# Agent attention and a maxout network: key turns in three parts, query turns in two, and head operations with places of their own

## The chip, the cores and the metric

The kernel runs on one core of a Trainium2 chip. The metric is device time in microseconds; the median of eight runs of the kernel before is 454.28 us (453.96 to 456.04).

## The reference

```python
def _attn_ref(q, k, v, agents):          # q, k, v: 4 x 12544 x 128; agents: 4 x 49 x 128
    def sm(a, b): ...                    # softmax(scale * a @ b^T) over the last axis
    a2k = sm(agents, k)
    agent_v = a2k @ v                    # 4 x 49 x 128
    q2a = sm(q, agents)                  # 4 x 12544 x 49
    return q2a @ agent_v

def _moe_ref(x, w1, w2, w3, w_out):      # x: 50176 x 128; w1..w3: 128 x 768; w_out: 768 x 128
    h = np.maximum(np.maximum(x @ w1, x @ w2), x @ w3)
    return h @ w_out
```

Everything is float32 outside; the kernel works in bfloat16 inside.

## The kernel before

For each of the four batches the kernel first goes through all keys and values (98 tiles of 128 rows, in eleven groups of nine or eight tiles) and sums exponentials and weighted values for the 49 agents. From the normalised sums `av` it makes a matrix G: agent values times the weights' differences w2 - w1 (columns from C21 = 0) and w3 - w1 (columns from C31 = 768; one block of 128 of them, the fourth, takes w3 - w2 instead), and a linear part through w1 and w_out. Then it goes through the queries, in 49 groups of 1024 rows. A query group is cast, turned, multiplied with the agents and exponentiated to `e_q`. For each of six blocks f of the hidden layer there is a first product u (`uv_ps`), a relu of it on ACT (`a_sb`, line 677), a second product v and a maximum of both on DVE (`r`, line 687); for f = 4 (FI) the two products are summed in one buffer and ACT does both steps (lines 674 and 685). Out of the six r tiles and w_out come the output's two halves (`o_ps`, lines 692 and 701), which DVE scales (line 708) and SP stores (line 715).

The order is written out by hand. Every operation is put into a list with a place, `at(place, fn)`; the list is sorted, and in that order the instructions are issued, so that each engine's queue is the sorted list cut down to its own instructions. A query group takes six place units. KEY holds the places of a group's steps relative to its start (6 s), LATE those of the groups from 36 on, OWN those of single groups, BORDER those around the change of batch, BATCH0 and BATCH3 those of a batch's last steps. Names: `u0` to `u5`, `v0` to `v5` products, `a` relus, `x` maxima, `oc` and `lin` output products, `sc` scaling, `st` store, `qt` and `qe` a query turn on PE and its evacuation, `s` and `ex` query scores and exponentials, `ks`, `ke`, `kv`, `ka`, `ea` the key group's scores, exponentials, values and sums.

Batch 0's keys and values are worked off in the head (function `head`), before any query group. There SP loads key group g at place g and value group g at g + 3.3; POOL casts a key group (line 378), PE turns it (365), DVE evacuates (368), PE takes scores (354), ACT exponentiates (359) and casts values (383), PE adds totals (395) and values (405), and from the third group on issues four matmuls that keep it busy (`warm(WARM)`, line 328). After the last key scores come twelve more (LAST_WARM), the differences of the weights (294), `av` (409), and G's two products (485) with their evacuations (418 on DVE, 420 on ACT). The places of the head are moved to the query groups' scale by adding HEAD_END - Z, about -16.32, so the head ends at 0.66.

The keys and values of batches 1 to 3 are worked off beside the query groups, one key group with each (function `k_group`). SP loads them, POOL casts them, and SP turns the keys through the DMA (`turn_k`, line 502); a few query groups (the last of each batch and all from 36 on) are turned through the DMA too (line 633). The places of loads, casts and turns come from STREAM, relative to 11 units ahead of the group (LEAD):

```python
STREAM = {"kl": 0.0, "ld": 0.5, "kc": 1.0, "qc": 1.5, "vl": 1.9, "kt": 2.0, "vc": 3.2}
...
z = 6.0 * s - LEAD + x
K[n] = (z if z > HEAD_END else HEAD_END + 0.001 * (s + x / 6.0)) - 6.0 * s
```

`kl`, `ld` and `vl` are the loads of keys, queries and values, `kc`, `qc` and `vc` their casts, `kt` the turn. What would fall into the head is put right behind it. Group 0's query load has place 13.15 on the head's scale, behind all but the last value load, and its cast 14.6, behind all key casts. SP issues all loads, DMA turns and stores (but the load of the agents) in one queue; after the first seven loads, all issued by 4.42 us, the next follows at 5.78, as earlier ones land.

Of the kernel before, what the change touches and what calls it, by code (L numbers as in the profile page):

```python
# [10 lines left out]
BF16 = mybir.dt.bfloat16  # L11
# [17 lines left out]
    "s": -2.94209, "ex": -2.10461, "u1": -0.58526, "a1": -0.11108, "u2": 2.13391, "a2": 3.22306,  # L29
    "v1": 3.39126, "u3": 3.76716, "x1": 4.61365, "v2": 4.65907, "u0": 4.68062, "a3": 4.76358,  # L30
    "x2": 4.9054, "a0": 5.15584, "v0": 5.44974, "u4": 5.62746, "x0": 6.09964, "a4": 6.12388,
    "u5": 6.27862, "v3": 6.63325, "a5": 6.82242, "v4": 6.98304, "x4": 6.98433, "lin1": 7.02719,
    "oc12": 7.03328, "sum": 7.23728, "oc10": 7.59283, "x3": 7.74792, "v5": 7.87225, "rec": 8.46283,
    "x5": 9.47889, "oc13": 9.6877, "oc11": 9.69832, "oc14": 10.58762, "oc15": 10.856, "lin0": 10.87306,
    "oc05": 11.17012, "sc1": 11.55345, "oc01": 11.72189, "oc00": 11.77009, "oc03": 11.79963,
    "oc02": 11.90624, "oc04": 11.95959, "sc0": 12.74339, "st": 15.47059,
# [3 lines left out]
        "u2": 0.64554, "u0": 0.6497, "a0": 0.75101, "a2": 0.92875, "sum": 1.27525, "u3": 2.06003,  # L40
        "v0": 2.59116, "x0": 2.68446, "a3": 2.85638, "rec": 2.96325, "u1": 3.03882, "v2": 3.6736,
        "u4": 4.24684, "a1": 4.93475, "x2": 5.01871, "v3": 5.81978, "u5": 5.84299, "a4": 5.908,
        "a5": 6.60823, "x3": 6.61479, "v4": 6.9759, "v5": 7.08557, "x4": 7.15158, "v1": 7.27894,
        "x5": 7.66161, "x1": 7.70792, "lin0": 9.14279, "oc05": 10.43605, "oc00": 10.7932, "oc02": 10.85481,
        "oc03": 11.37967, "oc01": 11.41219, "oc04": 11.66746, "sc0": 11.83826, "lin1": 12.49398,
        "oc10": 12.50239, "oc11": 12.59233, "oc12": 12.77266, "oc13": 12.88978, "oc14": 13.54796,
        "oc15": 13.60373, "sc1": 13.75975, "st": 20.17439,
    },
    1: {
        "qt": -4.60541, "qe": -4.48042, "s": -2.95099, "ex": -1.32724, "ks": 1.62294, "u0": 1.73602,  # L50
        "ke": 2.36058, "sum": 2.56616, "kv": 2.79082, "a0": 2.92319, "ka": 3.26757, "u2": 3.4201,
        "v0": 3.45964, "a2": 3.84717, "u3": 4.22117, "rec": 4.22129, "x0": 4.49406, "a3": 4.56793,
        "u1": 4.62522, "v2": 4.63012, "x2": 4.73195, "a1": 4.86854, "v3": 5.12545, "u4": 5.25359,
        "x3": 5.55542, "ea": 5.62671, "a4": 5.96399, "u5": 6.17953, "a5": 6.26476, "v1": 6.28947,
        "x1": 6.30399, "v4": 6.40498, "v5": 6.63853, "x5": 6.88027, "x4": 7.41578, "lin0": 8.99321,
        "oc00": 9.79175, "oc04": 10.56667, "oc02": 10.75084, "oc03": 11.28772, "oc01": 11.5494,
        "oc05": 11.68913, "sc0": 12.27589, "lin1": 12.53566, "oc13": 12.60573, "oc15": 12.61178,
        "oc10": 12.70709, "oc14": 13.24775, "oc12": 13.54581, "oc11": 13.80424, "sc1": 14.02652,
        "st": 19.02898,
    },  # L60
    34: {
        "qt": -2.58866, "qe": -1.82932, "s": -1.30778, "ex": -1.10174, "ks": 0.14415, "sum": 0.55608,
        "rec": 0.59015, "ke": 0.68278, "u0": 0.7058, "ea": 0.72143, "u2": 1.49989, "a0": 2.15219,
        "v0": 2.18384, "x0": 2.25012, "kv": 2.57078, "a2": 2.84672, "ka": 3.10787, "u3": 3.14749,
        "a3": 3.82134, "u1": 3.94172, "v3": 3.96473, "a1": 4.22804, "x3": 4.34837, "v2": 4.43956,
        "u4": 4.5536, "u5": 4.96643, "a4": 5.32988, "x2": 5.54314, "a5": 6.22364, "v4": 6.22498,
        "v1": 6.372, "x4": 6.51691, "v5": 6.61382, "x1": 6.73976, "x5": 6.95861, "lin1": 8.28778,
        "oc15": 8.36021, "lin0": 8.73553, "oc13": 9.18722, "oc04": 9.72211, "oc14": 10.51955,
        "oc01": 10.73827, "oc02": 10.8464, "oc03": 12.33286, "oc05": 12.39876, "oc00": 12.40014,
        "oc11": 12.72237, "sc0": 13.30654, "oc12": 14.30997, "oc10": 14.62572, "sc1": 14.9543,  # L70
        "st": 25.03309,
    },
    35: {
        "qt": -2.43671, "qe": -1.9414, "s": -1.5744, "ex": -1.28805, "ks": -1.09088, "ke": -0.64495,
        "sum": -0.18909, "kv": -0.10783, "ka": 0.5331, "rec": 0.56684, "u0": 0.82589, "a0": 0.91902,
        "u2": 1.00358, "v0": 1.49877, "x0": 1.58537, "a2": 2.26288, "u3": 2.5102, "v2": 2.57899,
        "x2": 3.98475, "u1": 4.05488, "a3": 4.05504, "v3": 4.37636, "a1": 4.49639, "u5": 4.62208,
        "x3": 4.92789, "a5": 5.44572, "v5": 5.48263, "x5": 5.93851, "u4": 7.30642, "a4": 8.24488,
        "v1": 8.30836, "x1": 8.49394, "lin0": 8.71742, "oc03": 8.91263, "oc02": 9.07857, "v4": 9.24912,
        "x4": 9.32541, "oc00": 9.39236, "oc04": 9.69131, "oc01": 10.88106, "lin1": 10.92225,  # L80
        "oc05": 11.01981, "oc15": 11.13488, "sc0": 11.61665, "oc12": 11.69455, "oc13": 11.87736,
        "oc14": 13.32657, "oc10": 13.37252, "oc11": 13.49981, "sc1": 13.74093, "st": 42.57773,
    },
    36: {
        "s": -4.45673, "ex": -3.49789, "u1": -0.09348, "a1": 2.12897, "u2": 2.20348, "a2": 2.77677,
        "v2": 3.2876, "u0": 3.526, "v1": 3.8727, "x2": 4.34512, "x1": 4.34975, "u3": 4.36198,
        "a0": 4.73186, "a3": 5.00514, "v0": 5.29756, "u4": 5.75498, "x0": 5.91535, "sum": 6.0162,
        "a4": 6.30588, "v3": 6.39331, "x3": 6.48929, "u5": 6.75132, "rec": 7.30888, "a5": 7.33831,
        "v4": 7.78698, "v5": 7.80684, "x5": 7.96407, "x4": 8.12232, "lin1": 9.0675, "oc12": 9.24639,
        "oc14": 9.95322, "oc10": 10.40131, "lin0": 10.43281, "oc04": 10.55626, "oc01": 10.64608,  # L90
        "oc11": 11.24862, "oc15": 12.02168, "oc13": 12.20592, "oc00": 12.38398, "oc03": 12.91102,
        "sc1": 12.98528, "oc02": 14.0029, "oc05": 14.08645, "sc0": 14.96085, "st": 29.7755,
    },
    37: {
        "s": -2.47874, "ex": -1.87009, "u1": -0.70419, "a1": -0.60046, "u2": 2.0221, "a2": 2.21078,
        "v2": 3.56807, "x2": 3.92118, "u0": 4.2218, "v1": 4.32407, "x1": 4.92454, "a0": 5.43373,
        "v0": 5.83985, "u3": 6.06605, "x0": 6.29959, "u5": 6.46966, "v3": 6.48031, "a3": 6.91113,
        "a5": 7.46701, "u4": 7.96938, "sum": 8.00459, "x3": 8.25588, "rec": 8.25634, "v5": 8.35007,
        "lin1": 8.44693, "oc11": 8.49987, "a4": 8.62997, "oc13": 8.8661, "v4": 9.25227, "x5": 9.45205,
        "oc12": 9.91769, "x4": 10.00657, "oc10": 10.0531, "lin0": 10.26202, "oc15": 10.56081,  # L100
        "oc14": 10.87787, "oc04": 10.95601, "oc05": 11.15532, "sc1": 11.49682, "oc01": 11.77199,
        "oc02": 11.78318, "oc00": 11.81904, "oc03": 12.16132, "sc0": 13.17137, "st": 43.83189,
    },
    47: {
        "s": -2.63303, "ex": -1.35705, "u1": -0.72334, "a1": -0.55161, "u2": 2.09887, "a2": 2.6128,
        "v1": 2.71229, "u3": 4.07931, "v2": 4.23837, "a3": 4.51758, "x1": 4.63092, "u0": 4.71212,
        "a0": 5.0718, "x2": 5.13888, "u4": 5.22695, "v0": 5.2509, "x0": 5.96934, "u5": 6.00235,
        "a4": 6.49548, "v3": 6.59342, "v4": 6.61016, "sum": 6.94315, "lin0": 6.95342, "x3": 6.98518,
        "a5": 7.11094, "oc00": 7.22404, "oc02": 7.24709, "v5": 7.29105, "rec": 7.33314, "x4": 7.43763,
        "lin1": 7.62467, "oc03": 7.73819, "oc11": 7.80383, "x5": 7.80889, "oc14": 8.24845, "oc12": 8.30273,  # L110
        "oc04": 8.48507, "oc10": 10.74469, "oc01": 11.20725, "oc05": 11.70935, "sc0": 11.81857,
        "oc15": 11.86159, "oc13": 12.01123, "sc1": 12.03976, "st": 16.08395,
    },
    48: {
        "s": -2.45577, "ex": -1.62439, "u1": -0.82051, "a1": -0.04899, "u2": 1.5047, "v1": 1.68501,
        "a2": 1.84167, "u0": 1.85869, "v2": 2.12726, "a0": 2.96358, "x1": 3.66201, "x2": 3.71048,
# [53 lines left out]
    },  # L170
}
BATCH0 = {
    "red": -0.0796, "tot": 0.34012, "nrm": 0.77389, "p31": 0.90693, "p21": 1.22633,
}
BATCH3 = {
    "red": -1.41636, "tot": -0.09802, "nrm": 0.57786, "p31": 0.95637, "p21": 1.99854,
# [4 lines left out]
def kernel(  # L181
# [26 lines left out]
    GT = 8  # L208
# [626 lines left out]
```

## Time and profile before

| | |
|---|---|
| median of eight runs | 454.28 us |
| the profiled execution, its own time | 456.04 us |
| its span, first to last instruction | 453.7 us (453.66) |
| busy share: PE, DVE, ACT, POOL | 96%, 89%, 88%, 37% |
| DMA queue 1's packets, share of 16 engines' time | 85.7% |
| first product of batch 0's G on PE | at 41.74 us |
| first maximum (r) on DVE | at 47.58 us |
| a query group from then on, with and without a key group | 8.15 and 7.71 us |

PE is TensorE, DVE VectorE, ACT ScalarE, POOL GpSimd, SP SyncE, PEld TensorE's weight loads. A row of the time line gives start and duration in us, the engine, the line and operation, out<-in with partitions x elements and type, the count, and in brackets the idle time before it and what ended that. A row of the waits gives the waiting engine and line, whom it waited for, the total in us, the times and the longest.

### The profile page before, as it was taken

How to read it: one execution, taken by the hardware profiler on the slowest of the kernel's cores; microseconds unless marked ns; L12 is line 12 of the kernel's file. 1: busy time of each engine (PE TensorE's matmuls, PEld its weight loads, DVE VectorE, ACT ScalarE, POOL GpSimd, SP SyncE). 2: the span in 40 equal slices, each digit the busy share in tenths (PEclk: the TensorE clock that was granted, in tenths of full speed). 3: DMA queues.
4: the chain of work that ended last, by engine and by line, in shares of the span. 5: the costliest groups of instructions: out<-in, count | busy, mean ns of one | idle time of the engine just before them, and what ended most of it. 6: DMA issues, size and time to landing. Idle time of an engine off the chain costs nothing.

```text
span 453.7 us, 13313 instructions
## 1 busy us (share of the span) xinstructions
PE 433.9 (96%) x5506; PEld 279.1 (62%) x5506; DVE 404.5 (89%) x505; ACT 398.4 (88%) x456; POOL 169.5 (37%) x165
## 2 busy tenths in 40 slices
PE   2988999999999999999999999999999999999995
PEld 2864566666665666666665666666665556565664
DVE  3324799999999999999999999999999999999995
ACT  1665899999998999999988999999989899999983
POOL 4335365556324354464423354544401101111000
PEclk9999999999999999999999999999999999999999
DMA  8999899898879989999799999999566666654933
GB/s 313 410 409 327 269 294 231 294 283 270 236 243 327 304 268 284 317 330 259 215 307 296 257 345 274 303 335 272 178 209 157 192 174 185 179 168 135 349 140 140
DMA packets 83655, 118.86 MB, mean 262 GB/s; under 512 B 57671, under 2 KB 59659, under 8 KB 83595
## 3 DMA queue, kind: packets, MB, share of 16 engines
q1 hardware_dynamic: 83392, 117.92, 85.7%
q8 instruction: 43, 0.70, 0.6%
q14 instruction: 17, 0.14, 0.1%
q10 hardware_dynamic: 203, 0.10, 0.1%
HBM read 78.74 MB, written 25.69 MB: 230 GB/s over the span
## 4 chain that ended last, share of the span: by engine, by line
PE 85%; DMA 8%; DVE 4%; issue 1%; ACT 1%; POOL 0%; DVEq 0%; SPq 0%
PE uv_ps L662 35%; PE o_ps L701 32%; PE o_ps L692 6%; DMA st<-in_k_dram 5%; PE m_ps L639 3%; PE m_ps L625 3%; DMA st<-in_q_dram 2%; DVE r L687 2%; PE m_ps L514 2%; PE m_ps L354 2%; DMA ag_st<-in_agents_dram 1%; PE m_ps L650 1%; PE uv_ps L485 1%; DVE o_sb L708 1%; PE o_ps L788 0%
## 5 line engine op out<-in xcount | busy, mean ns | idle before, releaser
L687 DVE TENSOR_TENSOR r<-uv_ps,a_sb 128x1024 bf16<-128x1024 f32 x245 | 297.5, 1222 | 10.5 <-PE uv_ps L662 5.5
L677 ACT ACTIVATE a_sb<-uv_ps 128x1024 bf16<-128x1024 f32 x245 | 242.9, 1024 | 20.2 <-PE uv_ps L662 16.9
L662 PE MATMUL uv_ps<-e_q,G 49*128 49x512 bf16 (+1 forms) x1248 | 182.6, 370 | 2.5 <-ACT G L420 1.0
L701 PE MATMUL o_ps<-wo_bf,r 128*128 128x128 bf16 x2352 | 179.1, 220 | 0.0
L701 PEld LDWEIGHTS <-r 128*128 128x128 bf16 x2352 | 139.8, 98 | 45.2 <-issue 42.2
L662 PEld LDWEIGHTS <-G 49*128 49x128 bf16 x1248 | 57.2, 94 | 63.4 <-issue 25.4
L620 POOL CAST q_bf<-st 128x1024 bf16<-128x1024 f32 x49 | 51.0, 1040 | 102.3 <-DMA st<-in_q_dram 82.3
L708 DVE TENSOR_TENSOR o_sb<-o_ps,recips 128x512 f32<-128x512 f32 x98 | 67.0, 685 | 2.9 <-PE o_ps L701 1.5
L498 POOL CAST v_bf<-st 128x1152 bf16<-128x1152 f32 (+1 forms) x33 | 37.5, 1137 | 47.8 <-DMA st<-in_v_dram 45.1
L685 ACT ACTIVATE r<-uv_ps 128x1024 bf16<-128x1024 f32 x49 | 50.3, 1026 | 1.3 <-PE uv_ps L662 0.6
L494 POOL CAST k_bf<-st 128x1152 bf16<-128x1152 f32 (+1 forms) x33 | 37.5, 1137 | 36.2 <-DMA st<-in_k_dram 36.2
L674 ACT ACTIVATE uv_ps<-uv_ps 128x1024 f32<-128x1024 f32 x49 | 49.6, 1011 | 0.9 <-PE uv_ps L662 0.6
L526 POOL TENSOR_TENSOR Eacc<-Eacc,e_k 128x441 f32<-128x441 f32 x27 | 27.7, 1024 | 39.7 <-ACT e_k L359 38.3
L692 PE MATMUL o_ps<-G,e_q 128*128 128x256 bf16 x196 | 37.9, 275 | 0.0
L645 ACT ACTIVATE e_q<-m_ps 128x512 bf16<-128x512 f32 x49 | 29.2, 597 | 2.3 <-PE m_ps L639 1.2
L629 DVE COPY qT<-m_ps 128x1024 bf16<-128x1024 bf16 x34 | 23.3, 686 | 3.4 <-PE m_ps L625 3.4
L368 DVE COPY kT<-uv_ps 128x1152 bf16<-128x1152 bf16 (+1 forms) x11 | 8.3, 752 | 17.2 <-PE uv_ps L365 17.2
L692 PEld LDWEIGHTS <-e_q 128*128 128x128 bf16 x196 | 12.1, 97 | 18.3 <-issue 18.1
L625 PE MATMUL m_ps<-ident,q_bf 128*128 128x128 bf16 x272 | 21.2, 222 | 0.1
L639 PE MATMUL m_ps<-qT,agT 128*64 128x512 bf16 (+1 forms) x104 | 19.9, 389 | 0.6 <-DVE qT L629 0.6
L378 POOL CAST k_bf<-st 128x1152 bf16<-128x1152 f32 (+1 forms) x11 | 12.5, 1137 | 17.9 <-DMA st<-in_k_dram 17.9
L383 ACT ACTIVATE v_bf<-st 128x1152 bf16<-128x1152 f32 (+1 forms) x11 | 12.2, 1112 | 7.9 <-DMA st<-in_v_dram 7.9
(73 smaller groups left out, 233.4 us busy)
## 6 DMA issues: line engine op xcount, KB each, us to landing
st<-in_q_dram SPq DMA_DIRECT2D x48, 512.0 KB, 5.5
out_dram<-o_sb SPq DMA_DIRECT2D x48, 512.0 KB, 5.4
st<-in_k_dram SPq DMA_DIRECT2D x40, 576.0 KB, 5.5
st<-in_v_dram SPq DMA_DIRECT2D x40, 576.0 KB, 8.6
st<-in_k_dram SPq DMA_DIRECT2D x4, 512.0 KB, 3.8
st<-in_v_dram SPq DMA_DIRECT2D x4, 512.0 KB, 6.7
st<-in_moe_w_dram SPq DMA_DIRECT2D x3, 384.0 KB, 10.7
kT<-k_bf SPq DMA_TRANSPOSE x33, 4.2
```

Of the source, the lines that this page charges most:

```text
L494: nc.gpsimd.tensor_copy(out=d["kb"][:, :n, :], in_=d["k"][:, :n, :])
L498: nc.gpsimd.tensor_copy(out=d["vb"][:, :n, :], in_=d["v"][:, :n, :])
L620: nc.gpsimd.tensor_copy(out=d["qb"], in_=d["q"])
L625: nc.tensor.transpose(t[:, j * P:(j + 1) * P], d["qb"][:, j, :], ident)
L662: nc.tensor.matmul(t[:, h, j0 * P:j1 * P], G[b][h * H:h * H + A, col + f * P:col + (f + 1) * P], d["e"][h * H:h * H + A, j0 * P:j1 * P], s ...
L674: nc.scalar.activation(u, u, AF.Relu)
L677: nc.scalar.activation(a_sb[f], u, AF.Relu)
L685: nc.scalar.activation(r, v_ps[f], AF.Relu)
L687: nc.vector.tensor_tensor(out=r, in0=v_ps[f], in1=a_sb[f], op=ALU.max)
L692: nc.tensor.matmul(t[:, i * 2 * C:(i + 1) * 2 * C], d["e"][:, jj * P:(jj + 1) * P], G[batch[jj]][:, C1O:C1O + 2 * C], start=(i == 0), stop ...
L701: nc.tensor.matmul(t[:, c:c + C], r_sb[f][:, h, jj * P:(jj + 1) * P], wo_bf[:, f, :], start=False, stop=True, skip_group_check=True)
L708: nc.vector.tensor_tensor(out=d["out"][:, j:j + m, :], in0=d["o", o].rearrange("p (j c) -> p j c", c=C), in1=d["r"][:, j:j + m].unsqueeze( ...
```

## The change

Key turns go through the DMA in three transfers instead of one, at places of their own; query turns by the DMA go in two. STREAM is now relative to the group's start and holds for every group: key loads at -16 instead of -11, key casts at -14 instead of -10, the three turns at -10.4, -9.95 and -9 with the query load before and the value load between them; nothing is held back to the head's end any more. Groups 0, 1 and 2 have places of their own for loads, casts and turns. The head's single operations have places in HEAD (relative to the place of the last key group, 13 on the head's scale). The weights: w3 is loaded right behind key load 1, the last 256 columns of w2 and all of w1 ahead of key load 6, the first 512 columns of w2 behind the last values. Query 0 is loaded behind key load 5 and cast ahead of key cast 3. LAST_WARM stands before the scores of key group 8. w2 - w1 is made on DVE alone, in two parts, and the evacuations of G's products have places of their own, the w3 part in two pieces on ACT for all batches. OWN, BORDER, BATCH0, BATCH3 and LATE have new values; KEY is the same.

```diff
+HEAD = {
+    "wl2": -11.95775, "wl1": -7.66522, "wl0": -7.00016, "w1c": -2.96197, "df": -2.63283,
+    "d21b": -2.16516, "wrm": -0.87406, "wl1b": 0.64663, "d31": 1.40444, "wol": 3.17448, "rcp": 3.42607,
+    "d21a": 3.71019, "nrm": 3.94714, "p31": 4.00522, "p21": 4.04405, "e31a": 4.05579, "e31b": 4.06804,
+    "e21b": 4.46718, "e21a": 5.31734, "woc": 6.19661, "w1t": 8.79656, "pli": 11.44809, "lin": 12.66141,
+}
+STREAM = {
+    "kl": -16, "kc": -14, "ld": -10.5, "kt0": -10.4, "kt1": -9.95, "qc": -9.5, "vl": -9.1, "kt2": -9,
+    "qd0": -8.95, "qd1": -8.45, "vc": -7.8,
+}
 OWN = {
     0: {
...
+        "ld": -11.22746, "qc": -10.38907, "qt": -6.32237, "qe": -5.87362, "s": -5.34845,
...
     1: {
...
+        "ld": -7.93803, "kl": -7.91068, "vl": -7.01176, "qc": -5.42752, "kc": -5.2794, "kt0": -5.26207,
+        "vc": -4.96613, "kt2": -4.66934, "kt1": -4.27484, "qt": -3.2266, "qe": -1.10869, "s": 0.42495,
...
+    2: {
+        "kl": -13.87399, "kc": -10.95348, "ld": -10.11466, "kt0": -8.29036, "qc": -8.07793,
+        "kt2": -7.5516, "kt1": -7.16622, "vl": -6.52325, "vc": -4.56598,
+    },
...
-    def load_w(i):
-        wst[i] = load_tile().rearrange("p j c -> p (j c)")[:, :Dff]
-        nc.sync.dma_start(wst[i], (moe_w1, moe_w2, moe_w3)[i])
+    def load_w(i, c0=0, c1=Dff):
+        if i not in wst:
+            wst[i] = load_tile().rearrange("p j c -> p (j c)")[:, :Dff]
+        nc.sync.dma_start(wst[i][:, c0:c1], (moe_w1, moe_w2, moe_w3)[i][:, c0:c1])
...
-    def differences_21():
-        difference(nc.vector, C21, 1, 0, slice(0, Dff // 2))
-        difference(nc.gpsimd, C21, 1, 0, slice(Dff // 2, Dff))
+    def difference_21(cols):
+        difference(nc.vector, C21, 1, 0, cols)
...
-            if g == NK + 1:
-                at(t + 0.1, lambda: load_w(0))
-                at(t + 0.2, lambda: load_w(2))
...
-        at(t - 0.65, lambda: load_w(1))
...
+        at(z + HEAD["wl0"], lambda: load_w(0))
+        at(z + HEAD["wl2"], lambda: load_w(2))
+        at(z + HEAD["wl1"], lambda: load_w(1, FI * P, Dff))
+        at(z + HEAD["wl1b"], lambda: load_w(1, 0, FI * P))
...
+        at(z + HEAD["p31"], lambda: product(C31))
+        at(z + HEAD["e31a"], lambda: evacuate(C31, 0, 2 * P))
+        at(z + HEAD["e31b"], lambda: evacuate(C31, 2 * P, Dff))
+        at(z + HEAD["p21"], lambda: product(C21))
+        at(z + HEAD["e21a"], lambda: evacuate(C21, 0, 2 * P))
+        at(z + HEAD["e21b"], lambda: evacuate(C21, 2 * P, Dff))
...
-        def turn_k():
-            d["kT"] = bf_tile("kT", 3)
-            nc.sync.dma_start_transpose(out=d["kT"][:, :n, :], in_=d["kb"][:, :n, :].rearrange("p j c -> p (j c)"))
+        def turn_k(i):
+            if i == 0:
+                d["kT"] = bf_tile("kT", 3)
+            j0, j1 = i * n // 3, (i + 1) * n // 3
+            nc.sync.dma_start_transpose(out=d["kT"][:, j0:j1, :],
+                                        in_=d["kb"][:, j0:j1, :].rearrange("p j c -> p (j c)"))
...
+        def turn_by_dma(i):
+            if i == 0:
+                d["qT"] = work.tile([P, GT, P], BF16, tag="qT", bufs=3, name="qT")
+            j0, j1 = i * n // 2, (i + 1) * n // 2
...
-        for n, x in STREAM.items():
-            z = 6.0 * s - LEAD + x
-            K[n] = (z if z > HEAD_END else HEAD_END + 0.001 * (s + x / 6.0)) - 6.0 * s
+        K.update(STREAM)
```

## The prediction

> **What bounds the kernel now.** I read the busy time by stage first, cut at the events that the change touches:
>
> ```profile
> 20.00:41.74 21.74, 18.88 (x305) 12.95 (x303) 8.16 (x14) 12.75 (x16) 7.13 (x7) 1.00 1.02 409
> 41.74:47.58 5.84, 4.87 (x38) 2.49 (x38) 2.13 (x5) 3.31 (x5) 3.38 (x3) 0.71 0.82 137
> 47.58:62.74 15.16, 14.58 (x184) 8.97 (x183) 13.81 (x18) 14.76 (x19) 7.35 (x7) 1.00 0.94 291
> 62.74:120.00 57.26, 57.26 (x760) 37.66 (x759) 56.55 (x71) 54.28 (x63) 33.70 (x33) 1.00 0.93 273
> ```
>
> After the stretch's bounds and length the columns are busy us of PE, PEld, DVE, ACT, POOL, then the granted clock, the DMA share, GB/s. Until 41.74 (first product of batch 0) the loads run at 409 GB/s: the head waits for memory. From 62.74 PE is busy all the time and DVE for 56.55 of 57.26: a query group takes 8.15 us (spacing of line 645's rows), and no load has a part in that. Between lies the ramp, 5.84 us without a single r tile.
>
> Then the time line of the head, POOL and PE, and the first steps on DVE:
>
> ```profile
> 9.98 1.15 POOL L378 CAST k_bf<-st 128x1152 bf16<-128x1152 f32 x1 [0.37 <-DMA st<-in_k_dram]
> ...
> 18.57 1.15 POOL L378 CAST k_bf<-st 128x1152 bf16<-128x1152 f32 x1 [1.71 <-DMA st<-in_k_dram]
> ...
> 38.14 1.04 POOL L620 CAST q_bf<-st 128x1024 bf16<-128x1024 f32 x1 [6.42 <-DMA st<-in_q_dram]
> ```
>
> ```profile
> 9.47 1.14 PE L365 MATMUL uv_ps<-ident,k_bf 128*128 128x128 bf16 x9
> ...
> 21.28 0.39 PE L354 MATMUL uv_ps<-agT,kT 128*128 128x49 bf16 x9
> 21.51 0.66 PE L365 MATMUL uv_ps<-ident,k_bf 128*128 128x128 bf16 x9
> ...
> 23.34 0.39 PE L354 MATMUL uv_ps<-agT,kT 128*128 128x49 bf16 x9
> ...
> 36.41 2.75 PE L328 MATMUL uv_ps<-ident 128*128 128x512 bf16 x12
> ...
> 41.74 0.52 PE L485 MATMUL uv_ps<-wall,avT 128*64 128x512 bf16 x4 [0.39 <-DVE avT L409]
> ```
>
> ```profile
> 47.58 1.22 DVE L687 TENSOR_TENSOR r<-uv_ps,a_sb 128x1024 bf16<-128x1024 f32 x1 [0.35 <-PE uv_ps L662]
> ```
>
> Key cast 3 runs at 9.98, cast 6 at 18.57: two 576 KB loads each 2.86 us. Query 0 is cast after all keys. Nine turns take 1.14 us early and 0.66 later: PE runs at half rate until 20.06. A round of PE (scores, turns, totals, values, four warming matmuls) is 23.34 - 21.28 = 2.06 us, shorter than the 2.86 between keys, so PE waits for loads and LAST_WARM's twelve fill a wait.
>
> Last, SP's own waits:
>
> ```profile
> SPq L502 <- POOL q_bf L620: 146.7, 25, 8.7
> SPq L633 <- POOL q_bf L620: 74.2, 15, 7.7
> ```
>
> SP stands 146.7 us before key turns, with loads behind them in its queue. But in all waits PE loses only about 3 us to casts (q_bf 1.8 + 0.8, Eacc 0.5). This standing is covered.
>
> **Steady part: nothing.** Key loads 5 place units sooner (6.8 us at 8.15 us for 6 units), 66 more key turns, 15 more query turns, loads between them. KEY's order on PE, DVE and ACT is untouched, LATE's engine orders are the same to a swap or two among line 701's steps, so the 8.15 and 7.71 us periods stay. Cover: SP issues per group one turn (1.30), two key/value loads, a query load and a store (0.58 + 0.43 + 0.45 + 0.38), 3.1 us of 8.15. If each third costs as much to issue as a whole turn, it is 5.7 us, in a turned query group 1.24 more: still hidden. Lower end none; the upper end is a third that lands one after the other, 3 x 4.2 = 12.6 us per group; the 6.8 us of earlier loading and SP's standing speak for the lower, which I take. The Trainium skill ("DMA: Bandwidth & Descriptors", "Rules for kernel authors") speaks against the cut: many small transfers should be made one large one. By its reason, fixed cost per transfer, 81 more would be a loss; the row of 4.2 us for a whole 288 KB turn and PE's full rows say that it is hidden here.
>
> **Head: the query cast blocks POOL.** Here I expect the change to hurt. Query 0's load goes behind key load 5, its cast (place -10.39) just ahead of key cast 3 (-10.32). POOL works in order. Query 0 is then the tenth load: 8 x 576 + 384 (w3, now after key 1) + 512 = 5504 KB. The ten loads before key cast 6 are 5760 KB and 18.57 us; 256 KB less at 1.43 us per 576 KB gives 17.93. Query cast 1.04, key cast 3 1.15: key group 3 is cast by 20.12 instead of 11.13, and keys 4 and 5, landed long before, queue behind it; on PE turns 3 and everything after stand.
>
> PE's queue from 20.12 to the last key scores: two rounds without warming at half rate, 2 x 2.37 (9.47 to 11.84 us, spacing of L365), 4.74; six with, 6 x 2.06 = 12.4; query 0's turns and scores, now in the middle, 0.62 + 0.41 = 1.0; LAST_WARM, moved ahead of scores 8, 2.6 of its 2.75. Sum 20.7: 40.9. Behind them on ACT, in order, the last exps 0.50, value casts 9 and 10, 1.16 + 0.63; then values 0.38, normalise 0.20, 0.3 of handing over: first product at 44.0 against 41.74, +2.3. Lower end -0.3: PE is in time and value load 10, which lands 0.33 later (131 KB of w2 cut off behind it, 262 left), plus cast, values and normalise make it 41.4. Upper end +4.0: the record has PE's clock change at 20.06, 43.95 and 47.37, on a grid of 3.41 us; if the second round fills no whole step, full rate comes 3.41 us later and half of that, 1.7, is lost. The Trainium skill ("TensorE: Matmul & The Clock Gate", Part 1) says that this window runs freely and lies differently in each run; no row here shows a second run. I take +2.7, a quarter of the 1.7 on top.
>
> **Ramp: a gain.** From the first product the queue is shorter: w2 - w1 is ready, its product follows at once on PE, all on DVE in two parts, query 0's scores and exps are done, and PE does not fall to half rate (41.74:47.58 shows 0.71). Products 2 x 0.52, evacuations 1.0 on DVE, v0 0.4: first r at about +2.7 us from the first product instead of 5.84, 3.1 gained. Given back: query 1's evacuation (0.69) and w1's (0.56) now fall behind it on DVE, and DVE waits for ACT's relus (0.94 to 1.02 each): 1.4. Net -1.7, between -0.5 (ACT's fifteen steps with gaps) and -2.7 (DVE never waits).
>
> **The rest.** G's evacuation for the other batches is cut in two on ACT: three times about 2 x 0.60 - 1.02 = +0.2, at the borders where DVE has the work; cover gone it would be 0.5 in all. The re-ordered borders: up to 0.6 either way, taken as nothing. The end: the stores of groups 35 to 37, placed among the last, go earlier; the last four still follow the last line-708 step, -0.1 (0 to -0.5). Weight loads: one more issue, 0.33 us on SP, hidden because SP issues the head's loads some 10 us ahead (key load 5 at 5.78, its cast at 15.71).
>
> **Sum:** +2.7 - 1.7 - 0.1 = +0.9, and 0.1 of ACT's 0.5 makes +1.0. The profiled execution took 456.04 us (span 453.66 and 2.38 around it): 457.0. It is 1.76 above the median of the eight, 454.28; with the same step the median becomes 455.3.
>
> **Rivals.**
> *PE catches up (faster).* Rounds wait less than I think, the backlog is worked off before the last value load at 39.8. For it: 2.06 against 2.86 per round wins 0.8 in each of seven rounds, 5.6 of the 9 us lost; against: LAST_WARM and the query turns in the middle take 3.6 of it back. It decides if scores 10 are done by 37.9. Then -0.3 - 1.7 - 0.1 = -2.1: 452.2.
> *It cancels (same).* Backlog at its early end, +1.6, and the ramp's -1.7: 454.2.
> *Small turns (slower).* A third lands like a whole turn, loads come behind it, and the group period grows. It decides only past 8.15 us per group; 0.1 us in each of 33 key groups is 3.3: 457.6. Against: PE's rows without waits.
> *The order does nothing:* no key load sooner moves a stage that PE and DVE bound; this is already in the sum.
>
> **How the numbers follow.** Backlog outweighs 0.48, catch-up 0.27, cancelling 0.18, small turns 0.07. 0.2% is 0.9 us, about what a measurement of this kernel can tell from no change. Backlog's own range is 454.0 to 457.3; its chance splits into 0.36 slower, 0.10 same, 0.02 faster; catch-up 0.26 and 0.01. Faster 0.28, same 0.29, slower 0.43. The range takes in half of the catch-up case and all but the end of the slow ones: 452.0 to 457.3.
>
> **What would show it.** Right: POOL's query cast near 17.9 and key cast 3 after it; PE idle from about 14 to 20; first product near 44, first r under 3 us behind it; 8.15 and 7.71 us unchanged; clock 1.00 through the ramp; SP's standing before line 502 much less than 146.7. Wrong: key cast 3 near 11; first product before 42; a group period over 8.2; PE waiting for kT.

## The result, and the profile after

The changed kernel takes 459.35 us (median of 19 runs, 455.35 to 462.44) against 455.06 us of the kernel before beside it: ratio 1.0088, 95% interval 1.0073 to 1.0104. It is slower by 0.9%, some 4 us. The ratios in this document are formed from the fast runs of both kernels and not from the two medians; of the 19 the two longest (462.29 and 462.44 us) are slow ones and left out. The prediction was 455.3, a loss of 1.0 us, with a range that ended at 457.3. The profiled execution took 458.92 us, span 457.1; that of before 456.04, span 453.66.

Head and ramp first, in the changed kernel's time line of POOL, PE and DVE (start, duration, engine, line, operation; in brackets the idle time before it and what ended it):

```profile
17.66 1.04 POOL L658 CAST q_bf<-st 128x1024 bf16<-128x1024 f32 x1 [7.29 <-DMA st<-in_q_dram]
18.65 4.47 POOL L398 CAST k_bf<-st 128x1152 bf16<-128x1152 f32 x4
```

```profile
13.64 0.55 PE L374 MATMUL uv_ps<-agT,kT 128*128 128x49 bf16 x9 [0.47 <-DVE kT L388]
19.85 1.14 PE L385 MATMUL uv_ps<-ident,k_bf 128*128 128x128 bf16 x9 [5.65 <-POOL k_bf L398]
...
22.22 1.14 PE L385 MATMUL uv_ps<-ident,k_bf 128*128 128x128 bf16 x9
...
26.88 0.66 PE L385 MATMUL uv_ps<-ident,k_bf 128*128 128x128 bf16 x9
...
32.85 3.61 PE L348 MATMUL uv_ps<-ident 128*128 128x512 bf16 x16
...
44.05 0.84 PE L514 MATMUL uv_ps<-wall,avT 128*64 128x512 bf16 x8 [0.30 <-DVE avT L429]
```

```profile
46.54 1.23 DVE L728 TENSOR_TENSOR r<-uv_ps,a_sb 128x1024 bf16<-128x1024 f32 x1 [0.58 <-ACT a_sb L718]
```

POOL stands 7.29 us for query 0's load and then casts four keys in one go; PE idles 5.65 us for the first of them. The first product stands at 44.05 instead of 41.74, the first r tile 2.49 us behind it instead of 5.84. So far this is the predicted picture. The first two rounds behind the gap run at half rate, also as worked: nine turns take 1.14 us at 19.85 and 22.22, and 0.66 at 26.88. The record of the granted clock begins at 25.11 in this execution (20.06 in that of before), so the 1.00 that the next table gives for the stretch from 20.00 does not show this.

The windows of the changed kernel, cut at its own events, and then cut in the late part (bounds and length, busy us of PE, PEld, DVE, ACT, POOL, granted clock, DMA share, GB/s):

```profile
20.00:44.05 24.05, 22.90 (x383) 17.24 (x381) 9.62 (x17) 14.53 (x19) 10.07 (x10) 1.00 1.02 408
44.05:46.54 2.49, 2.37 (x22) 1.13 (x23) 1.09 (x4) 1.93 (x4) 0.94 (x2) 1.00 0.73 208
46.54:62.67 16.13, 15.76 (x198) 9.62 (x197) 14.70 (x18) 15.35 (x20) 7.76 (x8) 1.00 0.86 228
62.67:120.00 57.33, 57.33 (x762) 37.69 (x762) 56.65 (x72) 54.45 (x64) 33.20 (x31) 1.00 1.00 268
...
370.00:434.20 64.20, 61.63 (x661) 35.62 (x661) 59.35 (x65) 59.86 (x65) 8.32 (x8) 1.00 0.55 146
434.20:457.10 22.90, 18.11 (x274) 12.96 (x273) 15.87 (x18) 12.54 (x13) 0.00 (x0) 0.88 0.69 274
```

The same late part of the kernel before:

```profile
370.00:433.00 63.00, 62.91 (x676) 36.67 (x674) 59.72 (x66) 60.71 (x67) 7.30 (x8) 1.00 0.65 204
433.00:453.60 20.60, 15.71 (x263) 11.80 (x260) 15.38 (x18) 12.18 (x13) 0.00 (x0) 1.00 0.31 120
```

The steady part is as it was: PE busy all of 57.33 us, 8.15 us between the exps of most neighbouring groups. The difference is in the groups without keys, 37 to 48: PE was busy for 62.91 of 63.00 us there, now for 61.63 of 64.20, and behind them the clock is 0.88 instead of 1.00. The exps of groups 36 and 48 lie 95.12 us apart instead of 93.27; from group 48's to the end it is 22.63 instead of 20.91.

The first row of the chain that ended last, before and then after, shows what has come onto the path, and PE's waits from 370 to 436 us show for what:

```profile
PE 85%; DMA 8%; DVE 4%; issue 1%; ACT 1%; POOL 0%; DVEq 0%; SPq 0%
```

```profile
PE 67%; DMA 12%; SPq 6%; DVE 5%; issue 4%; POOL 3%; ACT 1%; POOLq 0%; DVEq 0%; ACTq 0%
```

```profile
PE m_ps L680 <- DMA qT<-q_bf: 2.3, 5, 1.0
```

The longest of these waits is the last, that of group 48, in PE's time line:

```profile
434.17 0.30 PE L680 MATMUL m_ps<-qT,agT 128*64 128x128 bf16 x4 [1.03 <-DMA qT<-q_bf]
```

These 2.3 us of PE waiting for turned queries (kernel before: no such row in this stretch) match the 2.2 us that groups 36 to 48 lost against the runs below in which the turns come in time.

Why they come late is read from SP and POOL in one round of the late part. The kernel before, SP and then POOL:

```profile
376.98 1.24 SPq L633 DMA_TRANSPOSE qT<-q_bf  x1
378.27 0.58 SPq L616 DMA_DIRECT2D st<-in_q_dram  x1
378.89 0.44 SPq L715 DMA_DIRECT2D out_dram<-o_sb  x1
383.99 1.24 SPq L633 DMA_TRANSPOSE qT<-q_bf  x1
```

```profile
382.92 1.04 POOL L620 CAST q_bf<-st 128x1024 bf16<-128x1024 f32 x1 [5.97 <-DMA st<-in_q_dram]
```

The changed kernel, SP and then POOL:

```profile
371.53 2.50 SPq L673 DMA_TRANSPOSE qT<-q_bf  x2
374.07 0.58 SPq L654 DMA_DIRECT2D st<-in_q_dram  x1
...
379.81 2.50 SPq L673 DMA_TRANSPOSE qT<-q_bf  x2
382.35 1.43 SPq L654 DMA_DIRECT2D st<-in_q_dram  x1
383.83 0.43 SPq L756 DMA_DIRECT2D out_dram<-o_sb  x1
388.76 2.50 SPq L673 DMA_TRANSPOSE qT<-q_bf  x2
391.30 0.58 SPq L654 DMA_DIRECT2D st<-in_q_dram  x1
```

```profile
378.74 1.04 POOL L658 CAST q_bf<-st 128x1024 bf16<-128x1024 f32 x1 [7.24 <-DMA st<-in_q_dram]
387.69 1.04 POOL L658 CAST q_bf<-st 128x1024 bf16<-128x1024 f32 x1 [7.91 <-DMA st<-in_q_dram]
```

The next load is issued behind a turn, lands, is cast, and only then can SP issue the next turn, on which it has been standing in order; the load after that waits behind it. This is a closed ring. Its length before: turn 1.29, load to cast 382.92 - 378.27 = 4.65, cast and hand-over 1.07, together 7.01 us. That is under the 7.71 us in which PE and DVE do a group, so the ring ran ahead and nobody waited. A half turn holds SP as long as a whole one: two take 2.50. With them the ring is 2.54 + 4.67 + 1.07 = 8.28 us (371.53 to 379.81); with a slower landing, 382.35 to 387.69, it is 8.95. Six of its seven rounds from 371.53 to 430.39 take over 7.71, their mean is 8.41, and the stage now goes at the ring's pace as soon as its reserve is spent. The reserve is the time from the start of a group's turn to its exps: 9.88 us for group 36, 4.12 for group 48, while in the kernel before it goes from 9.62 to 14.19.

### The profile page after: what moved, and what is told of

Same layout as the page of the kernel before. It is cut to its first block, busy times and chain, and to the rows that moved or that the text cites. A ratio compares the mean times of both kernels' runs of the same rounds, so it can differ in the third digit from the quotient of the medians.

```text
span 457.1 us, 13435 instructions
## 1 busy us (share of the span) xinstructions
PE 432.7 (95%) x5506; PEld 277.3 (61%) x5506; DVE 404.4 (88%) x506; ACT 397.8 (87%) x459; POOL 168.2 (37%) x164
## 4 chain that ended last, share of the span: by engine, by line
PE 67%; DMA 12%; SPq 6%; DVE 5%; issue 4%; POOL 3%; ACT 1%; POOLq 0%; DVEq 0%; ACTq 0%
PE uv_ps L703 25%; PE o_ps L742 23%; DMA st<-in_q_dram 10%; SPq L673 5%; PE o_ps L733 4%; DVE r L728 3%; PE m_ps L663 3%; PE m_ps L680 3%; POOL q_bf L658 2%; PE m_ps L546 2%; PE uv_ps L348 2%; PE m_ps L374 2%; DMA st<-in_k_dram 2%; DMA qT<-q_bf 1%; PE uv_ps L385 1%
## 5 line engine op out<-in xcount | busy, mean ns | idle before, releaser
L742 PE MATMUL o_ps<-wo_bf,r 128*128 128x128 bf16 x2352 | 176.8, 220 | 0.0
L523 POOL CAST k_bf<-st 128x1152 bf16<-128x1152 f32 (+1 forms) x33 | 37.8, 1145 | 36.6 <-DMA st<-in_k_dram 36.5
L379 ACT ACTIVATE e_k<-uv_ps 128x441 bf16<-128x441 f32 (+1 forms) x11 | 5.9, 538 | 21.6 <-PE uv_ps L374 21.6
L379 ACT ACTIVATE e_k<-m_ps 128x441 bf16<-128x441 f32 (+1 forms) x33 | 17.8, 539 | 2.1 <-PE m_ps L691 0.7
```

The lines of the kernel that those rows point to most:

```text
L523: nc.gpsimd.tensor_copy(out=d["kb"][:, :n, :], in_=d["k"][:, :n, :])
L742: nc.tensor.matmul(t[:, c:c + C], r_sb[f][:, h, jj * P:(jj + 1) * P], wo_bf[:, f, :], start=False, stop=True, skip_group_check=True)
```

## The experiments

Theory A: the halves of the query turns lengthen this ring past 7.71 us, and that is the whole loss. Theory B: the rest of the change costs it, the new head or the 66 more key turns on SP.

### Query turns whole, in the changed kernel

```diff
-            for i in range(2):
-                at(key + K[f"qd{i}"], lambda i=i: turn_by_dma(i))
+            at(key + K["qd0"], turn_by_dma)     # one transfer of all 8 blocks
```

> The changed kernel with the query turns by the DMA whole again (one transfer at the first half's place). Theory A (query ring): from group 37 on SP turns a group, only then loads the next query group, which POOL must have cast before SP can turn it; a half turn holds SP as long as a whole one (1.25 us), so the ring takes 8.2 us instead of 7.0 against PE's 7.71 and the end of the kernel waits. Whole turns bring back the waits of groups 44 to 48 and the half-rate clock behind them: 3 to 4 us faster than the changed kernel, within 1 us of the kernel before (ratio 0.998 to 1.002). Theory B (head and stream: the blocked POOL cast, the small key turns): nothing comes back, ratio 1.007 to 1.010.

Measured: 455.15 us, ratio 0.9998 (0.9978 to 1.0018). One edit gives back the whole loss, with the new head and the thirds still in.

### Query turns in halves, in the kernel before

```diff
-            at(key + K["kt"], turn_by_dma)
+            for i in range(2):
+                at(key + K["kt"] + 0.5 * i, lambda i=i: turn_by_dma(i))
```

> The kernel before with nothing but its query turns by the DMA in two halves, half a place unit apart. Theory A: before has 10.5 us in hand at group 48 (turn landed at 421.7, used at 432.2); 12 groups lose 1.26 us each, 15 us, so the end waits some 3 to 6 us: ratio 1.006 to 1.013. Theory B: no change, ratio 1.000.

Measured: 460.85 us, ratio 1.0123 (1.0084 to 1.0161). The halves alone, in a kernel with the old head and whole key turns, cost at least as much as the whole change (the two intervals overlap).

### Halves kept, late query loads issued sooner

```diff
         K.update(STREAM)
+        if s > LAST:
+            K["ld"] -= 4.5
```

> The changed kernel, query turns still in halves, but from group 37 on each query load 4.5 place units sooner, so that SP issues the next load ahead of a group's turns and the ring is open. Theory A: the halves then cost nothing; as fast as with whole turns, ratio to before 0.998 to 1.002, SP's issue time of the halves unchanged (2.5 us per group). If it were the small transfers themselves (contention, or the time to land), it would stay at 1.007 or more.

Measured: 455.14 us, ratio 1.0003 (0.9982 to 1.0024). SP's time line in this run:

```profile
377.69 2.50 SPq L673 DMA_TRANSPOSE qT<-q_bf  x2
380.23 0.58 SPq L654 DMA_DIRECT2D st<-in_q_dram  x1
385.40 2.50 SPq L673 DMA_TRANSPOSE qT<-q_bf  x2
387.94 0.58 SPq L654 DMA_DIRECT2D st<-in_q_dram  x1
```

The two half turns still take 2.50 us and the same bytes move, but a group's load now goes ahead of the turn of the group before it; the ring is open, and the turns come at 7.71 us exactly. So neither SP's busy time nor the traffic is the cause by itself: the halves cost something only in the order that puts turn, landing and cast end to end.

### Key turns whole, halves of the query turns kept

```diff
-        for i in range(3):
-            at(key + keys[f"kt{i}"], lambda i=i: turn_k(i))
+        at(key + keys["kt0"], turn_k)     # one transfer of all blocks
```

> The changed kernel with the key turns whole again (one transfer at the first third's place), query turns still in halves. Theory A: no change against the changed kernel beyond 0.5 us, ratio to before 1.007 to 1.010, because key turns end before group 36 and no stage waits for them. Theory B (small key turns cost): 2 to 3 us faster than the changed kernel.

Measured: 460.19 us, ratio 1.0099 (1.0066 to 1.0132). Taking away the 66 small key turns does not bring the loss back. Six kernels side by side (a round of the ring is the time between SP's query turns, from 366 us on; the two columns behind its mean are distances between the exps of the groups named; the kernel before took 455.06 us beside the changed kernel and 454.68 beside the four below it):

| kernel | rounds of the ring, us | mean | groups 40 to 44 | groups 36 to 48 | median, us |
|---|---|---|---|---|---|
| before | 5.92 to 8.31 | 6.93 | 30.85 | 93.27 | 455.06 |
| after | 7.44 to 9.54 | 8.41 | 30.86 | 95.12 | 459.35 |
| after, query turns whole | 6.23 to 8.55 | 7.35 | 30.85 | 92.93 | 455.15 |
| after, loads ahead | 7.71 (open) | 7.71 | 30.85 | 92.93 | 455.14 |
| before, halves | 7.25 to 9.08 | 8.16 | 34.37 | 99.70 | 460.85 |
| after, key turns whole | 7.77 to 9.94 | 8.43 | 33.27 | 98.82 | 460.19 |

The means sort the six: up to 7.71 nothing is lost, over it 2.2 to 6.4 us in these groups. Single long rounds are harmless: with query turns whole three are over 8 us, where a load took longer to its cast (381.13 to 387.33), and PE waits for no turn. The two kernels with halves and whole key turns lose more in these groups than the changed kernel. A longer ring is the smaller part of that: from the turn of group 36 to that of group 48 it is 101.99 us (before, halves) and 102.31 (key turns whole) against 100.88. The larger part is that they have less reserve to spend, 2.29 and 3.49 us against 5.76. From turn to exps they are down to 4.41 and 4.50 us at group 40 and go at 8.3 to 8.6 us a group from there, where the changed kernel still has 7.23 and goes at 7.71 until group 44. Why the thirds leave it more reserve was not tried.

### The head: query 0's cast in turn

Query turns whole in this and the next three, so that the ring does not hide what the head does.

```diff
-        "ld": -11.22746, "qc": -10.38907, "qt": -6.32237, "qe": -5.87362, "s": -5.34845,
+        "ld": -11.22746, "qc": -7.4, "qt": -6.32237, "qe": -5.87362, "s": -5.34845,
```

> The kernel after with each query turn as one transfer (the run with query turns whole took 455.15 us, 0.9998 of before), and query 0's cast moved in the order from ahead of key cast 3 to between key casts 5 and 6, where its load has landed, so POOL no longer stands with keys 3 to 5 behind it. Theory that the blocked POOL costs the head about 2 us: key cast 3 back near 11, first product at 41.5 to 42.5 us instead of 44.05, the whole 453.2 to 454.2 us, ratio 0.995 to 0.998. Rival, that the ramp is bound by the last loads (value 10, the second half of w2, w_out) and gives back whatever the head loses: first product sooner, but the exps of group 2 at the same 57.7 us and the whole at 455.0, ratio 0.999 to 1.001.

Measured: 455.78 us, ratio 1.0015 (0.9995 to 1.0036). POOL and PE of this run:

```profile
10.92 1.15 POOL L398 CAST k_bf<-st 128x1152 bf16<-128x1152 f32 x1 [0.40 <-DMA st<-in_k_dram]
```

```profile
42.62 0.84 PE L514 MATMUL uv_ps<-wall,avT 128*64 128x512 bf16 x8 [0.31 <-DVE avT L429]
...
54.46 0.62 PE L663 MATMUL m_ps<-ident,q_bf 128*128 128x128 bf16 x8 [0.99 <-POOL q_bf L658]
```

Key cast 3 is back at 10.92 and the first product 1.7 us sooner than with the cast in its new place (42.62 against 44.35). But the ramp gives it back: group 2's exps are 1.2 us ahead (56.77 against 57.96), group 10's only 0.24 (123.49 against 123.73), after a wait of PE for a query cast at 54.46 and steps of 8.62, 8.58 and 8.40 us. The whole is not shorter, as the rival said, but its picture does not fit: it kept group 2's exps at 57.7. The query cast that PE waits for comes at 53.36, after POOL has stood 4.03 us for its load, and hardly sooner than with query 0's cast in the new place (53.91). So what lies behind the first product is not set by it alone; that value 10, w2 or w_out bind it is not shown. The head of this run was not undisturbed either: POOL stands 3.94 us for key load 6 (cast at 22.80), PE works 1.49 of the 4 us from 20.00, and from 23.72 the clock is at half for 3.41 us.

### The head: the last warming matmuls late again

```diff
-    "d21b": -2.16516, "wrm": -0.87406, "wl1b": 0.64663, ...
+    "d21b": -2.16516, "wrm": 2.66, "wl1b": 0.64663, ...
```

> The kernel after with each query turn as one transfer, and the last warming matmuls (3.6 us of PE in the changed kernel, at 32.85) put back behind the last totals, as in the kernel before. Theory that PE's queue is what the first product waits for: the 2.6 to 3.6 us leave the path, first product at 41.5 to 43.0 instead of 44.05, the whole about 1 us under the run with query turns whole (454.2, ratio 0.997). Rival, that PE must be kept warm there: the granted clock drops before the first product, the head gains nothing and the ramp runs at half rate for up to 3.4 us, the whole 455 to 457. Third case, the ramp gives it back: 455.1.

Measured: 455.28 us, ratio 1.0001 (0.9989 to 1.0014). First product at 43.93 against 44.35, of which 0.2 is an earlier start of the whole head. The first theory's numbers did not come, but the run does not test it:

```profile
39.72 2.75 PE L348 MATMUL uv_ps<-ident 128*128 128x512 bf16 x12
42.31 0.39 PE L425 MATMUL m_ps<-e_k,v_bf 128*128 128x49 bf16 x9
```

At their new place the twelve matmuls still stand in PE's queue ahead of the last values, and PE is busy all of the 13.00 us from 28.00. ACT has the last value cast done at 40.53, so without them the values could have run some 1.8 us sooner (an estimate from 42.31 and 40.53). In the kernel before the same place, at 36.41, filled a wait for loads. What the head gains without them, and whether the ramp gives it back, was not tried.

### Both head edits together

> Both edits of the two runs before this one together: query 0's cast between key casts 5 and 6, and the last warming matmuls behind the last totals, each query turn as one transfer. If each of them takes something off the head, first product at 41.4 (the last value load's landing plus cast, values, normalise) and the whole 452.5 to 453.7, ratio 0.994 to 0.997; if the ramp is bound by the last loads, 455, ratio 1.000.

Measured: 455.43 us, ratio 1.0002 (0.9980 to 1.0025); first product at 44.57, not 41.4. The windows of this run show one reason:

```profile
22.00:28.00 6.00, 5.72 (x53) 3.65 (x54) 1.75 (x2) 2.86 (x5) 2.29 (x2) 0.50 1.02 411
28.00:33.00 5.00, 5.00 (x91) 3.59 (x90) 2.50 (x4) 3.71 (x5) 1.87 (x2) 0.95 1.02 409
```

The clock was at half for 6.83 us from 21.68 in this execution, and the twelve warming matmuls stand ahead of the last values again (2.75 us from 40.36). This shows one run's head only; the medians say that neither edit nor both bring anything.

### Key turns whole and keys loaded at the old distance

```diff
-    "kl": -16, "kc": -14, "ld": -10.5, "kt0": -10.4, ...
+    "kl": -11, "kc": -10, "ld": -10.5, "kt0": -9, ...     # and turn_k as one transfer
```

> The kernel after with query turns and key turns each as one transfer, and the key group's load, cast and turn back at the places of before (11, 10 and 9 units ahead instead of 16, 14 and 10.4): of the change only the head's order and the other small moves are left. Theory that the key part of the change (sooner loads, thirds, loads between) neither gains nor loses: as the run with query turns whole, 455.15 within 0.5 us, with SP again standing over 100 us before the key turns. Rival, that sooner key loads were a gain in the steady part that the halves of the query turns only covered: 0.1 us per key group, 456 to 458 us; or the thirds a small loss: 454 to 454.7.

Measured: 455.47 us, ratio 1.0025 (1.0004 to 1.0045), against 455.15 and 0.9998 with sooner keys in thirds. The profiled spans are equal, 453.65 and 453.66 us; groups 3 to 36 take 273.45 and 273.57. SP's own waits here:

```profile
SPq L531 <- POOL q_bf L654: 135.6, 23, 7.5
SPq L667 <- POOL q_bf L654: 72.3, 15, 8.5
```

and in the changed kernel:

```profile
SPq L673 <- POOL q_bf L658: 67.0, 14, 7.5
SPq L533 <- POOL k_bf L523: 38.2, 25, 6.1
```

Over 90 us less standing of SP before key turns in the changed kernel, and the steady part is no shorter: the key part of the change is hidden, in gain and in loss. This is read from the profiles; the whole times cannot tell the two kernels apart, since their intervals overlap.

### The end's orders alone

Beside what the expectation names, this run and the next have the loads and casts of group 2 at the changed kernel's places: SP issues its key load ahead of query 1's load.

> The kernel before with one part of the change alone: the orders of the end (LATE and the own places of groups 34 and up) as in the changed kernel; head, key places and whole turns as before. From the profiled runs so far groups 36 to 48 take 92.93 us with the new orders and turns in step (query turns whole, or loads ahead), 93.27 before, and the tail after group 48's exps 20.82 against 20.91: if these small gains are of the end's orders, they come here without the new head's cost: groups 36 to 48 in 92.9, the whole 0.4 us under before, ratio 0.998 to 1.000. Rival: they came with the sooner key loads or the border's cut evacuations, and this is before to 0.1 us, groups 36 to 48 in 93.2 to 93.3. Third case: the stores' new places (20.85 instead of 15.47 units behind) stand against the loads in the queue, and the ring lengthens as with halves: over 456.

Measured: 456.64 us, ratio 1.0035 (1.0017 to 1.0053), and a miss: the step from group 36 to 37 grew from 8.63 to 9.78 us. The border's own steps had stayed at their old places and, as it seems, no longer fitted the new orders around them (the step is 9.15 us in every run that has both new). Among other things the last batch's value sum is normalised just ahead of the last key group's addition (335.63 and 335.88 us), which is so left out of G. The number is that of the third case, its cause is not: the rounds of the ring have a mean of 6.96 us. The whole time says nothing of the end's orders.

### All but the head and the DMA part

LATE, the own places from group 34 on, BORDER, both BATCH lists and the evacuations in parts as changed; the rest as before, but for group 2's loads and casts.

> Everything of the change but its head and its DMA part: the orders of the end, of the borders between batches and the border's evacuations in parts as in the changed kernel; the head, the key groups' places and whole turns as before. Against the run with only the query turns whole (groups 3 to 36 in 273.57 us, 36 to 48 in 92.93, tail 20.82; before 273.59, 93.27, 20.91) it has the old head and the old key places. Theory that the re-ordered end brings 0.3 to 0.4 us whatever the head and the keys do: groups 36 to 48 in 92.9, the whole 0.4 us under before, ratio 0.998 to 1.000, and 0.0 to 1.0 us under the run with query turns whole. Rival: the orders of the end fit only the new places of loads and turns, and the whole is 455 or more, ratio 1.001 to 1.004.

Measured: 455.03 us, ratio 0.9992 (0.9964 to 1.0019). Groups 36 to 48 take 93.29 us here, as before (93.27), not 92.93. But the steps show where: groups 36 to 40 take 31.24 us, as with whole query turns in the changed kernel, against 31.58 before, so the 0.34 us come with the re-ordered end and borders and need no new key places. One single step, group 40 to 41 at 8.07 instead of 7.71, takes them back; PE waits 0.29 us for DVE in it, and why is open. No version beats the kernel before by more than its measurement can tell.

## Why the prediction was wrong

**The step that failed** is in the steady part: "If each third costs as much to issue as a whole turn, it is 5.7 us, in a turned query group 1.24 more: still hidden", and with it "the 8.15 and 7.71 us periods stay". The size of the term was right: a small turn does cost as much as a whole one, and the query turn got 1.25 us longer. The comparison was wrong. It set SP's summed issue time against the group's period, as if SP only had to have enough time left. SP was not short of time: it stood 67.0 us waiting for query casts. What has to fit under the period is the ring: turn, landing and cast, one behind the other. It was 7.01 us before, in plain sight in the trace, 0.70 under the 7.71; 1.25 more made it 8.28. The prediction showed the row that tells of this ring, SP's 74.2 us of standing before the query turns, and read it as cover, since PE's waits for casts were small. A wait that costs nothing says nothing of how near it is to costing.

The bill, from the profiled executions of the changed kernel and of the one with whole query turns: 95.12 - 92.93 = 2.19 us in groups 36 to 48, and 22.63 - 20.82 = 1.81 after group 48, together 4.0. Up to group 36 the changed kernel was 0.5 ahead there, so the spans differ by 3.5 us; the medians differ by 4.2. Of the second part the clock is the likely cause: after PE's wait of 1.03 us, which ends at 434.17, the record has 3.41 us at half rate from 434.71, 1.7 us of work. It fits that the mean granted clock is 0.995 or less in 14 of the 20 executions of the changed kernel and at least 0.997 in all twelve with whole query turns; where in those executions the clock fell is not kept. The step does not come with every late turn: the kernel before with halves had none, and a tail of 20.99.

**The rival "small turns"** had the right object and the wrong place: it put the price on key thirds landing late in a group of 8.15 us, and the chance at 0.07. Key thirds cost nothing that can be measured. The prediction set aside the rule of the Trainium skill that many small transfers should be made one large one ("DMA: Bandwidth & Descriptors", "Rules for kernel authors"). Here it would have helped with the query halves (1.0088 with them, 0.9998 without), but size by itself is not the cause: with the next load issued first the same halves cost nothing (1.0003), and the key thirds cost nothing either.

**Head, +2.7:** right in mechanism and size. POOL's query cast at 17.66 (predicted 17.9), key cast 3 behind it, PE restarted at 19.85 (20.12), last key scores done at 40.71 (40.9), first product 44.05 (44.0): +2.3 as worked. The 0.4 added for a lost clock step did not show: PE came to full rate at about 25.1, where the two rounds at half rate end in the sum (20.12 + 4.74 = 24.86), and not 3.41 us later. "PE catches up" did not come.

**Ramp, -1.7:** first r 2.49 us behind the first product (predicted 2.7), clock 1.00. Against the profiled run of before it gave all of the 2.3 back: group 2's exps at 57.66 against 57.74, group 3's at 66.03 against 65.89. That run of before had the ramp's half clock, and it is not in every run: with the same head and none of it (before, halves) group 3's exps are at 64.67. Against that the new head and ramp lose 1.4 us. In the last experiment, again the old head without the half clock, they are at 65.97: it came to its first product 0.6 us later, and PE waited 0.68 for query 1's cast, whose load stands behind group 2's key load in that run. The new head and ramp thus cost 0.1 to 1.4 us by these profiles. The forecast of +1.0 was worked out against the profiled run of before, and against that one it was 0.9 too high.

**The rest, -0.1:** groups 3 to 36 take 273.36 instead of 273.59 us. So up to group 36 the changed kernel was 0.1 us ahead of the profiled run of before; all of the loss lies behind.

**What was named as a sign of error**, "PE waiting for kT", was looked for at the wrong tile: it was qT, and in the other stage.

## What to carry to other kernels

Where a queue works in order, follow one resource round: issue, landing, the step that frees it, the next issue, and compare this length, not the queue's busy time, with the period of the engines. A queue that stands much and delays nobody may be 0.7 us from being the bound; a step added to it is paid in every group once the ring has passed the period and the reserve is spent. The cheap cure here was an order that opens the ring (the next load ahead of the turn that waits); it gave back as much as undoing the halves.

## What the runs showed of the hardware

A DMA turn held SP for about the same time at every size tried here: 1.24 us for a query's eight blocks, 2.50 for its two halves of four; key thirds of three blocks 1.18 to 1.21 where nothing else delayed them, whole key turns of nine from 1.24 up. These rows are the changed kernel's from 130 to 145 us:

```profile
129.84 2.50 SPq L673 DMA_TRANSPOSE qT<-q_bf  x2
133.08 1.18 SPq L533 DMA_TRANSPOSE kT<-k_bf  x1
...
142.68 1.19 SPq L533 DMA_TRANSPOSE kT<-k_bf  x1
144.53 1.21 SPq L533 DMA_TRANSPOSE kT<-k_bf  x1
```

And the half-rate stretches of TensorE's clock lie differently from run to run of the same head: 43.95 to 47.37 in the profiled run of before, none there in the kernel with the same head and halved query turns, and group 3's exps are 1.2 us apart between the two. Heads that are compared by one profile of each kernel are known no better than that here.
